# Turning the fifth and sixth chunk at other places, moving two decay tables, output copies of later groups on VectorE, and another order on GpSimd

## The chip, the cores and the metric

The kernel runs on one core of one Trainium2 chip. The metric is the device time of one execution in microseconds (us), here the median of several runs. Besides, one execution is taken by the hardware profiler; its span runs from the first to the last instruction, and its own run time is a little longer than its span.

The engines: TensorE (PE, with its weight loads as PEld), VectorE (DVE), ScalarE (ACT), GpSimd (POOL) and SyncE (SP). Each works through its own list of instructions in order. In this kernel POOL issues all loads that change type on the way (f32 in memory, bf16 on the core), and SP issues the transposing DMAs and the stores.

## The reference

`q`, `k` and `v` are [4 batches, 8 heads, 768 tokens, 64]. The first half is a recurrent retention layer, the second a feed-forward layer with the snake activation:

```python
for t in range(S):
    state = gamma * state + outer(k[:, :, t], v[:, :, t])
    y[:, :, t] = scale * (q[:, :, t] @ state)
x = y.transpose(0, 2, 1, 3).reshape(B * S, H * D)     # 3072 x 512
h = x @ w_in                                          # 512 -> 2048
g = h + sin(alpha * h) ** 2 / alpha
out = g @ w_out                                       # 2048 -> 512, f32
```

## The kernel before, in words

**Chunks and groups.** The 768 tokens of a batch are cut into 6 chunks of 128. A chunk's retention is a masked product of its own q, k, v plus q times the state that the chunks before left. The list `P` holds the 24 chunks in the order of work: first the first chunk of every batch (`e0` to `e3`, also P[0] to P[3]), then the five others of batch 0 (P[4] to P[8]), of batch 1 (P[9] to P[13]), and so on. Feed-forward work goes by groups of chunks: group 0 has four chunks (512 tokens), groups 1 to 10 have two (256 tokens). Group 1 is P[4] and P[5], group 2 is P[6] and P[7].

**Stages of a chunk.** q and k are needed with the head dimension on the partitions, so they are turned: by eight PE transposes and one copy (`stage_T`, L241, the copy at L249 on ACT or L251 on DVE), or by a transposing DMA on SP (`turn`, L253). `stage_A` (L259) makes the scores in the PSUM tile `pa` and masks them on DVE into `aT` (L269). `stage_M` (L288) multiplies the state (`s_bd`) and `aT` into `py`, and DVE writes `py` times a decay table `qg[:, c]` into the feed-forward input `xT` (L310). The table of the c-th chunk of a batch is made once by `decay_table(c)` (L213, DVE). `keep_S` (L283, ACT) copies the new state out of the tile `ps`. v is scaled by the decay of its place by `scale_v` (L133, the instruction at L137), on POOL for most chunks. Batches 1 to 3 take their chunks 1 to 5 from one long load each (`load_seq`: eight DMAs each for q, k and v, one per head), and do scores, mix and state in one go (`burst`, L398: PE lines L327, L337, L341, L354, L357, L366).

**Feed-forward slots.** A `Slot` (L411) is one 128-row piece of the hidden layer for a group (two pieces from group 1 on): PE fills `ph` (L425), ACT takes the sine (L428), ACT or DVE squares it (`sq`: L433 on ACT, L435 on DVE), and `add` (L438, L440 on DVE) writes the activation into `gT`. `ff_out` (L447, PE at L450) multiplies a finished piece of `gT` by `w_out` into the output tile `po`; after 16 pieces `take` (L455) copies `po` to `o_sb` (L462) and SP stores it (L463). The tile `o_sb` has three buffers.

**PSUM tags.** `ph`, `po` and some of the turned tiles share four buffers of the tag `mm`, given out in turn. A new tile waits until what read or wrote the buffer's last tile is done. `po` of group 0's first two token tiles has the tags `ps` and `ty`, of which there is one each; `pa` is a tag of its own with one buffer.

**What sets the order.** `tc.manual_schedule()` (L60): each engine's list is the order in which the source calls the operations. Group 0's slots (L594 to L667) are written out by hand, with the helper `F(ts, fs)` for output products of group 0's first two token tiles, and `fill(n)` for the next n output products of its other two. Then come POOL's loads and scalings (L670 to L698), then the rest of P[4] and P[5] (L700 to L708). From group 1 on, `phase` (L543) runs a group's eight slots: in slot n it makes the Slot and its square, does what the last attention step left over ("exit", "keep", "hand"), calls the attention work tied to (group, n) by `at` (L716), then `now.add()`, and then its share of the output products of the group before (four per slot; two in group 1). Attention bursts lie in slots 1 and 5 of groups 2 and later. An output tile is finished in slots 3 and 7.

Of the kernel before, what the change touches and what calls it, by code (L numbers as in the profile page):

```python
# [15 lines left out]
def kernel(  # L16
# [15 lines left out]
    nc = tc.nc  # L32
# [36 lines left out]
    def chunk_of(t, j):  # L69
        b, c = divmod(j, NCH)  # L70
        return t[b, :, c * C:(c + 1) * C, :].rearrange("h s d -> s h d")

    def load_chunk(j, names="qkv"):
        for name, src in (("q", q), ("k", k), ("v", v)):
            if name not in names:
                continue
            if name == "v":
                t = big.tile([128, H, D], BF16, name="vr", tag="vr", bufs=10)
            else:
                if ("qk", j) not in raw:  # L80
                    raw["qk", j] = big.tile([128, 2, H, D], BF16, name="qkr", tag="qkr", bufs=9)
                t = raw["qk", j][:, "qk".index(name)]
            nc.gpsimd.dma_start(out=t, in_=chunk_of(src, j))  # L83
            raw[name, j] = t

    def wide(j):
        return j >= NCH + 2 and j % NCH > 0

    def load_seq(bt, names="qkv"):

        cs = [c for c in range(NCH) if wide(bt * NCH + c)]
        nh = 2 * len(cs)
        if "q" in names:
            raw["seq", bt] = (big.tile([128, nh, 2, NP, D], BF16, name=f"qk_seq{bt}"),
                              big.tile([128, nh, NP, D], BF16, name=f"v_seq{bt}"))
        tqk, tv = raw["seq", bt]
        for name, src in (("q", q), ("k", k), ("v", v)):
            if name not in names:
                continue
            for h in range(H):  # L100
                r = slice(64 * (h // NP), 64 * (h // NP) + 64)
                o = tv[r, :, h % NP, :] if name == "v" else tqk[r, :, "qk".index(name), h % NP, :]
                nc.gpsimd.dma_start(out=o, in_=src[bt, h, cs[0] * C:, :].rearrange("(f i) d -> i f d", i=64))  # L103
        for i, c in enumerate(cs):
            j, f = bt * NCH + c, slice(2 * i, 2 * i + 2)
            raw["qk", j], raw["k", j], raw["v", j] = tqk[:, f], tqk[:, f, 1], tv[:, f]
# [26 lines left out]
    def scale_v(j, eng):  # L133
        t, by = raw["v", j], kg
        if wide(j):
            t, by = t.rearrange("i f p d -> i (f p) d"), kgq
        eng.tensor_mul(t, t, by[:, j % NCH, :, None].to_broadcast([128, H, D]))  # L137
# [74 lines left out]
    def decay_table(c):  # L212
        nc.vector.tensor_mul(qg[:, c], qg[:, 0], step[:, c, :, None].to_broadcast([128, NP, C]))  # L213
# [27 lines left out]
    def stage_T(j, eng=None, tag="ty"):  # L241
        pt = psum.tile([128, 2 * NP, 128], BF16, name="pt", tag=tag, bufs=4 if tag == "mm" else 1)
        st["qkT", j] = work.tile([128, 2 * NP, 128], BF16, name="qkT", tag="qkT", bufs=6)
        for i in range(2):
            for p in range(NP):
                nc.tensor.transpose(pt[:, i * NP + p, :],
                                    raw["qk"[i], j][:, 2 * p:2 * p + 2, :].rearrange("p h d -> p (h d)"), ident)
        if eng is nc.scalar:
            nc.scalar.copy(st["qkT", j], pt)  # L249
        else:  # L250
            nc.vector.tensor_copy(st["qkT", j], pt)  # L251

    def turn(j):  # L253

        st["qkT", j] = work.tile([128, 2 * NP, 128], BF16, name="qkT", tag="qkT", bufs=6)
        nc.sync.dma_start_transpose(out=st["qkT", j], in_=raw["qk", j].rearrange(
            "i a f p d -> i (a f p d)" if wide(j) else "i a h d -> i (a h d)"))

    def stage_A(j):  # L259
        qkT = st["qkT", j]  # L260
        pa = psum.tile([128, 2, NP, 128], F32, name="pa", tag="pa")
        for p in range(NP):
            for e in range(2):
                r = slice(64 * e, 64 * e + 64)
                nc.tensor.matmul(pa[:, e, p, :], qkT[r, NP + p, :], qkT[r, p, :],  # L265
                                 start=(p == 0), stop=True, skip_group_check=True)
        aT = work.tile([128, 2, NP, 128], BF16, name="aT", tag="aT", bufs=2)
        m = dec.rearrange("p e n t -> p (e n) t") if j % NCH == 0 else mask_bc
        nc.vector.tensor_mul(aT.rearrange("p e n t -> p (e n) t"), pa.rearrange("p e n t -> p (e n) t"), m)  # L269
        st["aT", j] = aT  # L270
# [12 lines left out]
    def keep_S(j, ps):  # L283
        for e in range(2):
            r = slice(64 * e, 64 * e + 64)
            nc.scalar.copy(s_bd[(j % NCH + 1) % 2][r, :, r], ps[r, :, :])  # L286
# [116 lines left out]
    def run(more, *kinds):  # L403
        for kind in kinds:
            if more and kind in more:
                more.pop(kind)()
# [37 lines left out]
    po = {}  # L444
# [10 lines left out]
    def take(g, ts):  # L455
        o_sb = work.tile([128, d_model], F32, name="o_sb", tag="o_sb", bufs=3)
        if (g, ts) == end:
            h = d_model // 2
            nc.vector.tensor_copy(o_sb[:, :h], po[g, ts][:, :h])
            nc.scalar.copy(o_sb[:, h:], po[g, ts][:, h:])  # L460
        else:
            nc.scalar.copy(o_sb, po[g, ts])  # L462
        nc.sync.dma_start(out=out_view[:, groups[g][ts], :], in_=o_sb)  # L463
# [79 lines left out]
    def phase(g, outs, att, nf=1, on_vector=()):  # L543


        no, done = len(outs), 0
        for n in range(FF // nf):
            more, fresh = rest[0], {}
            now = Slot(g, n * nf, nf=nf).sq("D" if n in on_vector else "A")
            run(more, "exit", "keep", "hand")  # L550
            for fn in att.get(n, ()):
                fresh.update(fn() or {})
            run(fresh, "mask")
            if fresh:
                rest[0] = fresh
            now.add()
            while done < no * (n + 1) * nf // FF:
                outs[done]()
                done += 1

    def T(j):
        return lambda: stage_T(j)

    def X(j):
        return lambda: turn(j)
# [7 lines left out]
    def SK(j):  # L573
        return lambda: keep_S(j, stage_S(j))
# [3 lines left out]
    P = order  # L578
    n3, n4 = 3 * C, 4 * C
    def F(ts, fs):  # L580
        for f in fs:
            for t in ts:
                ff_out(0, t, f)

    def early(f, tag="mm"):
        return Slot(0, f, (0, n3), tag=tag)
# [3 lines left out]
    def fill(n):  # L590
        for _ in range(n):
            outs.pop(0)()
# [10 lines left out]
    c = early(3)  # L603
# [11 lines left out]
    c = early(6)  # L615
# [24 lines left out]
    F((0, 1), (5,))  # L640
    a = Slot(0, 11)
    b.sq("D").add()
    decay_table(4)
    F((0, 1), (6, 7))
    b = Slot(0, 12)
    a.sq("A").add()
    decay_table(5)
    F((0, 1), (8,))
    a = Slot(0, 13)
    b.sq("D").add()  # L650
    F((0, 1), (9,))
    b = Slot(0, 14)
    a.sq("A").add()
    F((0, 1), (10,))
    a = Slot(0, 15)
    b.sq("D").add()
    F((0, 1), (11,))
    a.sq("A").add()
    stage_T(P[4], nc.scalar, "mm")
    F((0, 1), (12, 13))  # L660
    fill(2)
    stage_A(P[4])
    scale_v(P[4], nc.vector)
    F((0, 1), (14,))
    stage_T(P[5], nc.scalar, "mm")
    turn(P[6])
    F((0, 1), (15,))  # L667


    load_chunk(P[7])  # L670
    load_chunk(P[8], "qk")
    load_chunk(P[9], "qk")
    scale_v(P[6], nc.gpsimd)
    load_seq(1, "q")
    load_chunk(P[8], "v")
    scale_v(P[7], nc.gpsimd)
# [4 lines left out]
    scale_v(P[9], nc.gpsimd)  # L681
    load_seq(1, "v")
    scale_v(e2, nc.gpsimd)
    load_seq(2, "q")
    for j in P[10:12]:
        scale_v(j, nc.gpsimd)
    load_seq(2, "k")
    for j in P[12:14]:
        scale_v(j, nc.gpsimd)
# [7 lines left out]
        scale_v(j, nc.gpsimd)  # L697
    load_seq(3, "v")  # L698

    fill(1)  # L700
    stage_A(P[5])
    SK(e0)()
    scale_v(P[5], nc.vector)
    fill(5)
    stage_M(P[4])
    fill(4)
    stage_M(P[5])
# [8 lines left out]
    def at(place, fn):  # L716
        atts[place[0]].setdefault(place[1], []).append(fn)
# [8 lines left out]
    def B(old, new, first):  # L726
        return lambda: burst(old, new, first)

    at((1, 0), T(P[7]))
    for n in range(6, NJ + 1):  # L730
        new = P[n] if n < NJ else None
        first = new - 1 if n < NJ and new % NCH == 1 else None
        if n > 6 and wide(P[n - 1]):
            at(where[n], B(P[n - 1], new, first))
        else:
            if n > 6:
                at(where[n], lambda j=P[n - 1], last=wide(new): (M_last if last else stage_M)(j))
            at(where[n], lambda j=new: (scores if wide(j) else stage_A)(j))
            if first is not None:
                at(where[n], SK(first))  # L740
        if n + 2 < NJ:
            at(where[n], X(P[n + 2]))
        if n >= 19 and n < NJ:
            at(where[n], lambda j=new: scale_v(j, nc.gpsimd))
# [34 lines left out]
```

## Time and profile before

| | |
|---|---|
| median of 3 runs | 216.23 us (215.36 to 217.09) |
| the profiled execution: its time, its span | 216.35 us, 214.6 us |
| PE busy | 202.1 us (94%) |
| ACT busy | 167.6 us (78%) |
| DVE busy | 141.4 us (66%) |
| POOL busy | 107.2 us (50%) |
| granted PE clock | 1.00 throughout |
| ACT copies of output tiles, L462 | 23 of 0.571 us |
| POOL scalings, L137 | 21 of about 1.1 us |
| transposing DMAs of single chunks, from issue to landing | 8.6 us (median of 3) |

How to read it: a row of the timeline has the start, the length, the engine, the line, the operation, its tiles, and in brackets how long the engine had been idle and who ended that. A PE product's length is modelled to its end, and products overlap; the next product's start says more than the length of the one before. The list of waits adds up such idle times by pairs. The chain is followed back from the last instruction, at each step to what released it or to the instruction before it on its engine. The chain of this execution runs from the loads (POOL's issues, and DMAs of weights, q, k, v) over the scaling of `v_seq` at 81.50 us into PE, and stays on PE from 82.6 us to the last products.

### The profile page before, as it was taken

The page shows a single profiled execution, that of the slowest core. Times are in us where ns is not written, and L with a number is a line of the kernel's source. Part 1 is how long each engine was busy: PE and PEld are TensorE (multiplying, and loading weights), DVE is VectorE, ACT ScalarE, POOL GpSimd, SP SyncE. Part 2 cuts the span into 40 slices and gives each one's busy share as a digit, 9 for nine tenths or more (in the row PEclk, how much of TensorE's full clock was granted, in tenths as well). Part 3 has the DMA queues.
Part 4 walks back from the last instruction along what each step waited for, and adds up shares of the span by engine and source line. Part 5 has one row for each costly group of instructions (what it writes and reads, how often), then busy time and mean ns, then how long its engine had stood idle before and what let it go on. Part 6 is the DMA issues. An engine that isn't in the chain of part 4 may idle for free.

```text
span 214.6 us, 5482 instructions
## 1 busy us (share of the span) xinstructions
PE 202.1 (94%) x2171; PEld 134.5 (63%) x2197; DVE 141.4 (66%) x330; ACT 167.6 (78%) x365; POOL 107.2 (50%) x145
## 2 busy tenths in 40 slices
PE   7898899998999998999999999999999999999994
PEld 3444554456766666766766766666767667666654
DVE  4887859966896567477567568568576667555520
ACT  7688696757888986977977977977977877888841
POOL 8965433896879969999999500000330231000000
PEclk9999999999999999999999999999999999999999
DMA  9999999999998999999999913217304101100112
GB/s 130 150 194 186 206 207 169 154 127 216 160 139 72 153 175 188 157 130 200 164 124 169 151 33 101 73 25 101 93 11 101 49 3 50 52 28 21 49 53 98
DMA packets 101338, 25.01 MB, mean 117 GB/s; under 512 B 93872, under 2 KB 98368, under 8 KB 101312
## 3 DMA queue, kind: packets, MB, share of 16 engines
q0 software_dynamic: 77504, 13.38, 86.2%
q1 hardware_dynamic: 23664, 11.22, 24.8%
q8 instruction: 17, 0.28, 0.6%
q14 instruction: 9, 0.07, 0.1%
q10 hardware_dynamic: 144, 0.07, 0.1%
HBM read 27.27 MB, written 6.29 MB: 156 GB/s over the span
## 4 chain that ended last, share of the span: by engine, by line
PE 59%; DMA 25%; POOL 12%; issue 2%; DVE 0%; POOLq 0%; DVEq 0%
PE po L450 27%; PE ph L425 26%; DMA w_out<-in_moe_w_out_dram 8%; DMA w_in<-in_moe_w_in_dram 5%; DMA v_seq<-in_v_dram 4%; POOL qkr L83 4%; DMA qk_seq<-in_q_dram 4%; DMA qkr<-in_k_dram 4%; POOL v_seq L103 2%; POOL vr L83 2%; PE poh L473 2%; POOL vr L137 1%; PE py L327 1%; PE pa L337 1%; POOL qk_seq L103 1%
## 5 line engine op out<-in xcount | busy, mean ns | idle before, releaser
L440 DVE SCALAR_TENSOR_TENSOR gT<-s,rec_alpha,ph 128x256 bf16<-128x256 f32 (+3 forms) x184 | 82.2, 488 | 55.1 <-ACT s L433 54.7
L428 ACT ACTIVATE s<-ph,alpha_sb 128x256 f32<-128x256 f32 (+3 forms) x184 | 79.2, 480 | 28.8 <-PE ph L425 27.6
L425 PE MATMUL ph<-xT,w_in 128*128 128x256 bf16 (+3 forms) x735 | 98.6, 277 | 0.3 <-DVE gT L440 0.2
L450 PE MATMUL po<-w_out,gT 128*128 128x512 bf16 x344 | 90.3, 379 | 3.9 <-issue 3.2
L425 PEld LDWEIGHTS <-w_in 128*128 128x128 bf16 x736 | 70.5, 98 | 31.8 <-issue 2.8
L433 ACT ACTIVATE s<-s 128x512 f32<-128x512 f32 (+1 forms) x92 | 57.1, 621 | 2.5
L450 PEld LDWEIGHTS <-gT 128*128 128x128 bf16 x368 | 34.0, 98 | 26.4 <-issue 0.9
L391 POOL CAST s_bd<-s_f 64x256 bf16<-64x256 f32 x10 | 3.9, 394 | 50.3 <-DVE s_f L386 26.6
L103 POOL DMA_DIRECT2D qk_seq<-in_q_dram x24 | 17.1, 756 | 4.2 <-DMA v_seq<-in_v_dram 2.1
L103 POOL DMA_DIRECT2D qk_seq<-in_k_dram x24 | 17.0, 760 | 1.1 <-DMA qk_seq<-in_q_dram 0.9
L103 POOL DMA_DIRECT2D v_seq<-in_v_dram x24 | 17.1, 783 | 0.0
L137 POOL TENSOR_TENSOR v_seq<-v_seq,kgq 128x512 bf16<-128x512 bf16 x14 | 14.8, 1106 | 3.0 <-DMA v_seq<-in_v_dram 2.7
L462 ACT COPY o_sb<-po 128x512 f32<-128x512 f32 x23 | 13.0, 571 | 2.5 <-PE po L450 2.5
L346 DVE TENSOR_TENSOR aTw<-pa,maskq 128x768 bf16<-128x768 f32 x14 | 13.3, 949 | 0.0
L83 POOL DMA_DIRECT2D vr<-in_v_dram x10 | 9.3, 925 | 3.9 <-DMA w_in<-in_moe_w_in_dram 1.7
L492 PE MATMUL spare<-warm 128*128 128x512 bf16 x27 | 9.8, 487 | 1.3 <-DVE warm L156 1.2
L377 DVE TENSOR_TENSOR xT<-py,qg 128x256 bf16<-128x256 f32 x28 | 10.4, 414 | 0.0
L83 POOL DMA_DIRECT2D qkr<-in_k_dram x9 | 8.1, 899 | 4.6 <-DMA w_out<-in_moe_w_out_dram 3.3
L83 POOL DMA_DIRECT2D qkr<-in_q_dram x9 | 8.1, 897 | 3.9 <-DMA w_in<-in_moe_w_in_dram 1.7
L269 DVE TENSOR_TENSOR aT<-pa,mask 128x1024 bf16<-128x1024 f32 x6 | 7.3, 1217 | 0.7 <-PE pa L265 0.7
L137 POOL TENSOR_TENSOR vr<-vr,kg 128x512 bf16<-128x512 bf16 x7 | 7.5, 1091 | 0.1
L286 ACT CAST s_bd<-ps 64x256 bf16<-64x256 f32 x14 | 5.1, 361 | 2.2 <-PE ps L279 2.1
(92 smaller groups left out, 151.8 us busy)
## 6 DMA issues: line engine op xcount, KB each, us to landing
out_dram<-o_sb SPq DMA_DIRECT2D x23, 256.0 KB, 2.3
w_in<-in_moe_w_in_dram POOLq DMA_DIRECT2D x4, 512.0 KB, 11.7
w_out<-in_moe_w_out_dram POOLq DMA_DIRECT2D x4, 512.0 KB, 15.4
vr<-in_v_dram POOLq DMA_DIRECT2D x10, 128.0 KB, 6.9
qk_seq<-in_q_dram POOLq DMA_DIRECT2D x16, 80.0 KB, 5.6
qk_seq<-in_k_dram POOLq DMA_DIRECT2D x16, 80.0 KB, 3.6
v_seq<-in_v_dram POOLq DMA_DIRECT2D x16, 80.0 KB, 4.1
qkr<-in_q_dram POOLq DMA_DIRECT2D x9, 128.0 KB, 7.1
```

The source lines that it names most:

```text
L83: nc.gpsimd.dma_start(out=t, in_=chunk_of(src, j))
L103: nc.gpsimd.dma_start(out=o, in_=src[bt, h, cs[0] * C:, :].rearrange("(f i) d -> i f d", i=64))
L137: eng.tensor_mul(t, t, by[:, j % NCH, :, None].to_broadcast([128, H, D]))
L346: return {"mask": lambda: nc.vector.tensor_mul(aT, pa[:, :, 0:384].rearrange("p e (m t) -> p e m t", m=2), maskq[:, None, None, :].to_broa ...
L377: nc.vector.tensor_mul(x[:, 2 * b:2 * b + 2, :], py[b][:, 0:256].rearrange("p (m t) -> p m t", m=2), qg[:, c, 2 * b:2 * b + 2])
L425: nc.tensor.matmul(self.ph[:, m, :], w_in[:, i, f * 128:(f + 1) * 128], xT[g][:, i, self.lo:self.hi], start=(m == 0 and i == 0), stop=(i = ...
L428: nc.scalar.activation(out=self.s[:, m, :], in_=self.ph[:, m, :], func=ACTF.Sin, scale=alpha_sb[:, f:f + 1])
L433: nc.scalar.activation(out=self.s, in_=self.s, func=ACTF.Square)
L440: nc.vector.scalar_tensor_tensor(gT[self.g][:, f, self.lo:self.hi], self.s[:, m, :], rec_alpha[:, f:f + 1], self.ph[:, m, :], op0=ALU.mult ...
L450: nc.tensor.matmul(po[g, ts], gT[g][:, f, ts * C:(ts + 1) * C], w_out[:, f, :], start=(f == 0), stop=(f == FF - 1))
L462: nc.scalar.copy(o_sb, po[g, ts])
L492: nc.tensor.matmul(spare["ps"], warm[:, :128], warm, start=True, stop=True)
```

## The change

Six edits. (1) `take` copies the output tiles of groups 1 to 10 on DVE; those of group 0 stay on ACT, and the very last tile, which is copied in parts at L477 and L479, stays as it is. (2) In `phase`, `now.add()` stands behind the output products and not before them. (3) In group 0's last slots P[4] is turned one slot earlier, into a tile of the tag `pa`, its scores follow one slot later, and P[5] is turned before product 14; the `fill` calls and the scaling of P[4]'s v are placed anew. (4) `decay_table(4)` and `decay_table(5)` go from group 0's slots to slots 0 and 4 of group 1. (5) On POOL, P[6]'s v is scaled before the q and k of P[9] are loaded. (6) On POOL, P[10]'s v, the first of batch 1's long load, is scaled before the q of batch 2 is loaded, P[11]'s after it.

On PE no instruction is added or removed, only some in group 0's last slots change places. On ACT 19 copies go, on DVE 19 come.

```diff
@@ take
+        elif g > 0:
+            nc.vector.tensor_copy(o_sb, po[g, ts])
         else:
             nc.scalar.copy(o_sb, po[g, ts])
@@ phase
-            now.add()
             while done < no * (n + 1) * nf // FF:
                 outs[done]()
                 done += 1
+            now.add()
@@ group 0's last slots
     a = Slot(0, 11)
     b.sq("D").add()
-    decay_table(4)
     F((0, 1), (6, 7))
     b = Slot(0, 12)
     a.sq("A").add()
-    decay_table(5)
     F((0, 1), (8,))
...
     b = Slot(0, 14)
     a.sq("A").add()
-    F((0, 1), (10,))
+    F((0, 1), (10, 11))
+    stage_T(P[4], nc.scalar, "pa")
     a = Slot(0, 15)
     b.sq("D").add()
-    F((0, 1), (11,))
+    F((0, 1), (12,))
+    stage_A(P[4])
     a.sq("A").add()
-    stage_T(P[4], nc.scalar, "mm")
-    F((0, 1), (12, 13))
-    fill(2)
-    stage_A(P[4])
-    scale_v(P[4], nc.vector)
-    F((0, 1), (14,))
+    F((0, 1), (13,))
     stage_T(P[5], nc.scalar, "mm")
     turn(P[6])
+    F((0, 1), (14,))
+    fill(2)
     F((0, 1), (15,))
+    scale_v(P[4], nc.vector)
@@ GpSimd's order
     load_chunk(P[7])
     load_chunk(P[8], "qk")
+    scale_v(P[6], nc.gpsimd)
     load_chunk(P[9], "qk")
-    scale_v(P[6], nc.gpsimd)
     load_seq(1, "q")
...
     scale_v(e2, nc.gpsimd)
+    scale_v(P[10], nc.gpsimd)
     load_seq(2, "q")
-    for j in P[10:12]:
-        scale_v(j, nc.gpsimd)
+    scale_v(P[11], nc.gpsimd)
     load_seq(2, "k")
...
-    fill(1)
     stage_A(P[5])
+    fill(2)
     SK(e0)()
     scale_v(P[5], nc.vector)
-    fill(5)
+    fill(4)
     stage_M(P[4])
...
     at((1, 0), T(P[7]))
+    for c, n in ((4, 0), (5, 4)):
+        at((1, n), lambda c=c: decay_table(c))
```

## The prediction, as put on record

> **What bounds the kernel now.** I read the page first, then the waits of PE by stretch, then the chain, and last the timeline around each wait of PE.
>
> ```profile
> PE 202.1 (94%) x2171; PEld 134.5 (63%) x2197; DVE 141.4 (66%) x330; ACT 167.6 (78%) x365; POOL 107.2 (50%) x145
> PEclk9999999999999999999999999999999999999999
> ```
>
> PE is busy 94% of the span at full clock, and the change takes no product from it. So only idle time of PE can be won. Where it lies, for the stretch from 36 to 84 us (two lists, PE's products and its weight loads; the columns are total us, times, longest):
>
> ```profile
> PE pa L265 <- ACT qkT L249: 0.7, 2, 0.5
> PE pa L265 <- DMA qkT<-qkr: 0.5, 1, 0.5
> PE py L354 <- POOL v_seq L137: 0.4, 1, 0.4
> PE po L450 <- DVE gT L440: 0.2, 1, 0.2
> ...
> PEld L265 <- DMA qkT<-qkr: 0.7, 1, 0.7
> PEld L354 <- POOL v_seq L137: 0.5, 1, 0.5
> ```
>
> Four waits: for the copies of the turned P[4] and P[5], for P[6]'s transposing DMA, for P[10]'s scaled v, and for one `add`. After 84 us no such wait is left, but the chain shows a small regular one:
>
> ```profile
> 95.52 0.87 PE ph L425 x8
> 96.40 0.86 PE po L450 x4
> 97.26 0.98 PE ph L425 x8
> ```
>
> The third piece is 0.11 us longer than the first, though both are eight equal products. The timeline says why:
>
> ```profile
> 96.59 0.57 ACT L462 COPY o_sb<-po 128x512 f32<-128x512 f32 x1
> 96.71 0.87 DVE L440 SCALAR_TENSOR_TENSOR gT<-s,rec_alpha,ph 128x256 bf16<-128x256 f32 x2 [1.35 <-ACT s L433]
> ```
>
> ACT's copy of the finished output tile ends at 97.16 and the next `ph`, which gets that buffer, starts at 97.20. In the stretch 84 to 147 us the chain has eight such pieces, seven of 0.98 and one of 1.00: 0.90 us in all.
>
> Sums are against the profiled execution, 216.35 us (span 214.6 and 1.75 around it). It lies 0.12 us above the median, 216.23.
>
> **Part 1 and 2: output copies on DVE, `add` behind the products.** ACT loses 19 copies of 0.571 us (10.8 us), DVE gains 19. DVE's copy out of PSUM is not in the trace at this size; the nearest rows are the 128x256 copy at L720, 0.42 us (L720 in the timeline at 75.86), and the 128x512 product at L310, 0.69 us. I take 0.69, the same size: 13.1 us more on DVE, 141 to 154 of 214 us. The copy comes before the `add` of its slot in DVE's list, so it is seen against the row above: the tile's last product ends at about 95.5, DVE is idle from 95.4 to 96.7, the copy runs from 95.55 to 96.24 and still leaves the `add` at 96.71. At either price (0.42 or 0.69) it is done almost a microsecond before ACT's was, and the wait at 97.09 goes. Worth 0.90 us; bounds 0 (another release of that buffer is as late) and 0.90. A loss needs a copy longer than the 1.35 us of idle time that cover it; then `add`, and the buffers that it frees, come late. Moving `add` itself costs PE nothing, since in a slot the products of the group before do not read the `gT` that this `add` writes.
>
> [...]
>
> **Part 6: P[10]'s v scaled before batch 2's q is loaded.** POOL's row in the timeline:
>
> ```profile
> 80.78 0.71 POOL L103 DMA_DIRECT2D qk_seq<-in_q_dram  x1 [0.32 <-DMA v_seq<-in_v_dram]
> 81.50 2.05 POOL L137 TENSOR_TENSOR v_seq<-v_seq,kgq 128x512 bf16<-128x512 bf16 x2
> ```
>
> The last of batch 1's v lands at 80.49 by the trace; POOL then issues one more load (to 81.49), scales from 81.50 to 82.55, and PE, ready at 82.03, goes on at 82.61. With the scaling first it ends at about 80.5 + 1.06 = 81.6, before PE asks. That frees up to 0.57 us. Queued behind it on POOL: eight q issues of 0.71 us (81.6 to 87.3, before 73.4 to 81.5), P[11]'s scaling (to 88.4; PE asks at 90.6), eight k issues (to 94.1, before to 89.2), P[12]'s scaling (to 95.2; asked at 98.6). SP's turn of P[14] waits for that k, issued at 92.5 now and at about 97 to 98 then, with the store of 97.2 behind it; at 5.4 us like the next turn it lands by 103.5, and its scores are due at 106.4. Slack of 2 us or more everywhere, so I cost these at nothing; if the cover were gone PE would wait for the excess once.
>
> **Part 4: the two tables.** Each is 0.67 us of DVE (five at L213). Taken from 35.3 and 36.6, they let products 12 to 14 come earlier (part 3). Put into slot 0 of group 1, the first delays an `add` by 0.28 us and the mask of P[6] by 0.07: hidden. In slot 4 there is no room:
>
> ```profile
> 58.62 0.87 DVE L440 SCALAR_TENSOR_TENSOR gT<-s,rec_alpha,ph 128x256 bf16<-128x256 f32 x2 [0.28 <-ACT s L433]
> 59.41 0.68 DVE L435 TENSOR_TENSOR s<-s 128x512 f32<-128x512 f32 x1
> 60.13 0.87 DVE L440 SCALAR_TENSOR_TENSOR gT<-s,rec_alpha,ph 128x256 bf16<-128x256 f32 x2
> 60.92 0.68 DVE L310 TENSOR_TENSOR xT<-py,qg 128x512 bf16<-128x512 f32 x1
> 61.52 1.21 DVE L269 TENSOR_TENSOR aT<-pa,mask 128x1024 bf16<-128x1024 f32 x1
> 62.66 0.86 DVE L440 SCALAR_TENSOR_TENSOR gT<-s,rec_alpha,ph 128x256 bf16<-128x256 f32 x2
> ```
>
> DVE runs from 58.62 to 63.53 without a gap, and its last `add` there ends the wait of `po` at 63.57 (PE idle from 63.24). Of the table's 0.68 us, 0.28 fit into the idle time before 58.62; 0.40 reach that `add` and PE. Bounds 0 (PE has run ahead less) and 0.68. I take +0.40.
>
> **Part 3 and 5: P[4] and P[5], and P[6]'s v.** From 38.3 to 48.3 us PE waits about 1.1 us: 0.1 at P[4]'s turn, 0.2 at its scores, 0.6 at P[5]'s scores, 0.2 at the state. Worked out anew from rows: product 11 ends at 37.69; P[4]'s k lands at 38.03, so its turn ends at 38.3; Slot 15 to 39.16, product 12 to 39.6; the copy of 0.99 us from 38.5 lets the scores in at 39.6. Product 13 to 40.36; P[5]'s k lands at 40.91, its turn ends at 41.2, its copy at 42.4. Product 15 needs its `add`, now behind P[4]'s mask (1.22 us, from 40.4 to 41.6), so 42.35; scores of P[5] at 42.8; state from 43.7; `stage_M` at 45.06, where it is 45.03 now. New waits of 0.2 (k), 0.4 (k) and 0.35 (`add`), and one more change between product shapes (0.2), eat what is won. But this hardly matters: PE comes to P[6]'s scores at about 51.0 and waits until 51.51 for P[6]'s turn, issued at 43.73 when its k has landed and landed at 51.46. No edit moves that issue. What is won before it is lost there; up to 0.5 lost before it costs nothing. Bounds -0.5 (the turn lands that much earlier) and +0.3 (losses of 0.8). I take 0.
>
> POOL's scaling of P[6]'s v waits for its landing (44.53) and then takes 1.16 us, so P[9]'s q is issued at about 45.7, not 43.29, and batch 1's q at 47.4, not 46.23. Most of this is covered, as eight loads are in flight. I take 0 for the loads that follow; bound +1.2 us of lateness.
>
> **Sum.** At 82 us: PE comes 0.40 later (82.43) and finds v ready (81.6), so it is 0.18 ahead of 82.61. After that 0.90. 216.35 - 0.18 - 0.90 = 215.27, say 215.3.
>
> **Rivals.**
> - P[6]'s turn lands 0.5 us earlier, since P[9]'s loads are not yet beside it. For: it takes 7.7 us, the shortest turn 3.1. Against: its own issue stays, and other loads are queued. PE comes to 82 us at 81.93; the sum is -0.64 - 0.90 = 214.8. With the table's 0.40 hidden too, 214.4.
> - Slower: the whole load stream comes late, because POOL stands waiting for P[6]'s v. Lateness d shows where v of P[10] is scaled: ready at 81.6 + d. The point at which it eats all is 82.61 + 0.90 - 81.6 = 1.9 us. For: P[9]'s q is 2.4 us late. Against: batch 1's q is only 1.2 late, and the queue is full. At d = 2.4: 216.35 + 1.4 - 0.9 = 216.85.
> - The copies free nothing: `ph` waits as long for DVE. For: DVE takes the copies in order, and its square or mask may stand before them. Against: 1.35 us idle there. 216.35 - 0.18 = 216.2.
>
> **How the numbers follow.** Forecast 0.48, early turn 0.24, late loads 0.13, copies that free nothing 0.15. The range goes below 214.4 by the 0.5 that the table's and the turn's bounds leave, 213.9, and above 216.85 to 216.9. Within 1% (214.1 to 218.4) is about what a measurement of this kernel can tell from no change: its three runs spread over 1.7 us. Faster by more needs 2.2 us of the some 2.4 that all bounds give together: 0.10, from the early turn's tail and some of the forecast. Slower by more needs late loads beyond 3.5 us: 0.05. The rest, 0.85, is the same.
>
> **What would show it.** Right: no piece of 0.98 in the chain's `ph` after 84 us; copies at L462 on DVE that start when `po` is done; no wait of L354 for v. P[6]'s turn still awaited at 51.5. The wait of `po` for `gT` near 63.5 grown to about 0.6. Wrong: scores of P[6] well before 51, or waits at L303 or L354 for POOL; DVE's copies starting late, after a square; idle time of PE in batch 2's bursts from 106 us on.

## The result and the profile after

| | before | after |
|---|---|---|
| median | 215.86 us (8 runs, 215.18 to 217.09) | 214.41 us (8 runs, 213.81 to 215.42) |
| the profiled execution: time, span | 216.35, 214.6 us | 214.81, 213.0 us |
| PE starts P[6]'s scores (L265) | 51.51 us | 51.20 us |
| PE starts the `po` products that wait for `add` near 63 us (L450) | 63.57 us | 63.48 us |
| PE starts P[10]'s products of v (L354) | 82.61 us | 81.97 us |
| PE starts P[23]'s products of v (L354) | 185.90 us | 184.38 us |

The time is 0.9934 of before, 95% interval 0.9904 to 0.9963: about 1.4 us less. That is inside the 1% that the prediction called the same, though the interval does not reach 1. The two profiled executions differ by 1.54 us; the prediction's sum was 1.08. The rows of the table say where: 0.64 us until P[10]'s products of v, another 0.88 from there to P[23]'s.

The page of after, engines first. From L460 on its line numbers are higher by 2 (VectorE's copy is L462, ScalarE's L464, the store L465).

```profile
PE 201.3 (94%) x2171; PEld 134.3 (63%) x2197; DVE 155.1 (73%) x349; ACT 160.4 (75%) x346; POOL 107.2 (50%) x145
PE 72%; DMA 13%; DVE 7%; POOL 5%; issue 2%; POOLq 0%
```

VectorE has 13.7 us more; ScalarE has 7.2 less, not the 10.8 of its copies, since these overlapped their neighbours (in before the one at 96.59 by 0.20 us) and busy time counts that once; PE's share is as before. The second line is the head of the chain (followed back from the last instruction): VectorE now has 7% of it, in before 0%.

The chain of after in batch 2 (start, length, what), answering to the piece of 0.98 us shown for before:

```profile
93.02 0.87 PE ph L425 x8
93.89 0.86 PE po L450 x4
94.76 0.87 PE ph L425 x8
95.63 0.86 PE po L450 x4
96.49 0.87 PE ph L425 x8
```

And VectorE's timeline beside it:

```profile
94.79 0.69 DVE L462 COPY o_sb<-po 128x512 f32<-128x512 f32 x1 [0.19 <-PE po L450]
95.96 0.87 DVE L440 SCALAR_TENSOR_TENSOR gT<-s,rec_alpha,ph 128x256 bf16<-128x256 f32 x2 [0.47 <-ACT s L433]
```

The copy starts when the tile is finished, ends at 95.48, and the `ph` that takes its buffer, by the reading of before, starts at 96.33 without a wait. All pieces of `ph` in the stretch are 0.87.

The waits of PE's products between 36 and 84 us in after (us in total, times, longest):

```profile
PE po L450 <- issue: 1.3, 8, 0.2
PE pt L246 <- DMA qkr<-in_k_dram: 0.5, 1, 0.5
PE po L450 <- DVE gT L440: 0.4, 1, 0.4
```

Of before's waits, those for the copies of P[4] and P[5], for P[6]'s transposing DMA and for the scaled v are gone; a wait of 0.5 for P[4]'s k has come, and the one for `gT` has grown from 0.2 to 0.4. (The gaps marked "issue" are no waits; see the last section.)

The row of P[6]'s turn, in before and in after, by the view of DMAs of L256 between 42 and 46 us (the second line of each is the time from issue to landing):

```profile
L256 SPq DMA_TRANSPOSE qkT<-qkr x1: 1337/1337/1337, 43.7 to 43.7; - x1
...
DMA to landing us min/median/max: 7.7/7.7/7.7
```

```profile
L256 SPq DMA_TRANSPOSE qkT<-qkr x1: 1328/1328/1328, 43.9 to 43.9; - x1
...
DMA to landing us min/median/max: 5.4/5.4/5.4
```

It was issued 0.2 us later and landed 2.2 us earlier (49.30, not 51.46). And POOL's timeline ahead of P[10]'s products of v in after:

```profile
78.56 1.04 POOL L137 TENSOR_TENSOR v_seq<-v_seq,kgq 128x512 bf16<-128x512 bf16 x1 [5.48 <-ACT s L433]
79.55 5.76 POOL L103 DMA_DIRECT2D qk_seq<-in_q_dram  x8
```

POOL stood 5.5 us for the last of batch 1's v (landed 78.18, in before 80.49), scaled it by 79.6, and only then issued batch 2's q. The row names ScalarE as the one that ended the wait, but it was the load: POOL started 0.38 us after its landing here and 0.39 in early_act (landed 80.41, started 80.80).

### The profile page after: what moved, and what is told of

It is laid out like the page before. It is cut to its first block, busy times and chain, and to the rows that moved or that the text cites. A ratio compares the mean times of both kernels' runs of the same rounds, so it can differ in the third digit from the quotient of the medians.

```text
span 213.0 us, 5482 instructions
## 1 busy us (share of the span) xinstructions
PE 201.3 (94%) x2171; PEld 134.3 (63%) x2197; DVE 155.1 (73%) x349; ACT 160.4 (75%) x346; POOL 107.2 (50%) x145
## 4 chain that ended last, share of the span: by engine, by line
PE 72%; DMA 13%; DVE 7%; POOL 5%; issue 2%; POOLq 0%
PE po L450 32%; PE ph L425 30%; DMA qkr<-in_k_dram 8%; DMA w_in<-in_moe_w_in_dram 4%; DVE gT L440 3%; DVE aT L269 2%; POOL qkr L83 2%; PE poh L475 2%; PE pa L337 2%; PE py L327 1%; POOL vr L83 1%; PE py L366 1%; PE py L354 1%; POOL w_out L116 1%; PE py L299 1%
## 5 line engine op out<-in xcount | busy, mean ns | idle before, releaser
L450 PE MATMUL po<-w_out,gT 128*128 128x512 bf16 x344 | 90.5, 380 | 4.3 <-issue 3.3
L450 PEld LDWEIGHTS <-gT 128*128 128x128 bf16 x368 | 33.8, 98 | 27.0 <-issue 1.2
L462 DVE COPY o_sb<-po 128x512 f32<-128x512 f32 x19 | 13.1, 691 | 5.4 <-PE po L450 5.4
```

Source lines behind the costliest of these rows:

```text
L450: nc.tensor.matmul(po[g, ts], gT[g][:, f, ts * C:(ts + 1) * C], w_out[:, f, :], start=(f == 0), stop=(f == FF - 1))
L462: nc.vector.tensor_copy(o_sb, po[g, ts])
```

## The experiments

Twelve kernels, in three sets, each set on one chip with its own runs of before. Squares_beside, which changes the steady part itself, is left out of the table. One number sorts the others: the time from P[10]'s first product of v to P[23]'s (both L354), the steady part of the kernel, against the time up to it.

| kernel | of before, 95% interval | P[6]'s turn, us to landing | P[6]'s scores | P[10]'s v scaled | L354 of P[10] (waited) | to L354 of P[23] |
|---|---|---|---|---|---|---|
| before | | 7.7 | 51.51 | 82.56 | 82.61 (0.4) | 103.29 |
| after | 0.9934 [0.9904, 0.9963] | 5.4 | 51.20 | 79.61 | 81.97 | 102.41 |
| copies_only | 0.9957 [0.9926, 0.9988] | 8.0 | 50.98 | 79.64 | 82.44 | 102.40 |
| p10_first | 1.0004 [0.9972, 1.0035] | 7.8 | 51.26 | 80.88 | 81.81 | 103.27 |
| p6_first | 0.9971 [0.9950, 0.9993] | 5.5 | 50.99 | 80.21 | 81.53 | 103.28 |
| old_turns | 0.9926 [0.9899, 0.9953] | 5.6 | 50.98 | 78.35 | 81.53 | 102.40 |
| p9_first | 0.9931 [0.9904, 0.9958] | 8.1 | 51.17 | 81.41 | 82.03 | 102.41 |
| p10_back | 0.9911 [0.9885, 0.9938] | 5.6 | 50.82 | 79.92 | 81.59 | 102.41 |
| tables_early | 0.9898 [0.9867, 0.9930] | 5.6 | 51.28 | 80.37 | 81.83 | 102.41 |
| copy_add_ahead | 1.0137 [1.0108, 1.0166] | 5.5 | 50.83 | 78.71 | 81.71 | 107.13 |
| turns_tables | 0.9994 [0.9962, 1.0026] | 7.8 | 50.93 | 83.04 | 83.09 (1.2) | 103.32 |
| early_act | 0.9880 [0.9836, 0.9923] | 5.6 | 50.87 | 81.84 | 81.89 (0.4) | 102.43 |
| after_again | 0.9890 [0.9851, 0.9930] | 5.6 | 50.83 | 79.54 | 81.61 | 102.40 |

My theory after the result: the copies give their 0.9 in the steady part, and what is won before 82 us comes from the order on POOL, which lets P[6]'s turn land early, not from the new places of the turns. The rivals: the gain hangs together and cannot be taken apart, or the turning order carries it.

**The copies alone (copies_only).** Before, with these two edits:

```diff
+        elif g > 0:
+            nc.vector.tensor_copy(o_sb, po[g, ts])
...
-            now.add()
             while done < no * (n + 1) * nf // FF:
                 outs[done]()
                 done += 1
+            now.add()
```

> The kernel before with the output copies of the later groups on VectorE and add behind the products (parts 1 and 2), nothing else. Theory (the three gains are separate and add up): the pieces of 0.98 us of eight ph products after 84 us become 0.87, the wait for the scaled v at 82.6 us stays, and the span goes from 214.6 to 213.7 us (0.90 less). Rival (the whole gain of 1.5 us hangs on the order of POOL, and the copies only shift the wait): 214.3 to 214.6 us, with pieces of 0.98 or longer waits of PE for gT elsewhere.

Measured: 215.05 us against 216.01, profiled span 213.5. The theory holds for the steady part, 103.29 down to 102.40. The wait for the scaled v, which the theory expected to stay, was not there: in this execution v was ready at 79.64 in the old order. A new loss stood elsewhere, in the chain from 53 to 60 us:

```profile
53.20 0.47 ACT s L428
53.67 0.02 issue
53.70 1.99 DVE s L435
55.69 0.03 issue
55.71 0.87 DVE gT L440 x2
...
59.15 1.04 PE ph L425 x8
```

A square on VectorE took 1.98 us instead of 0.69, and the `ph` at 59.15 waited 0.9 us for it. POOL's timeline of the same kernel has the neighbour:

```profile
53.15 0.90 POOL L83 DMA_DIRECT2D vr<-in_v_dram  x1
54.07 1.05 POOL L137 TENSOR_TENSOR vr<-vr,kg 128x512 bf16<-128x512 bf16 x1
```

It is taken up under squares_beside.

**P[10] first, alone (p10_first).** Before, with `scale_v(P[10], nc.gpsimd)` ahead of `load_seq(2, "q")` and P[11]'s after it.

> The kernel before with one edit: P[10]'s v is scaled before batch 2's q is issued (part 6). Theory A (the last load of batch 1's v lands 2.3 us earlier, at about 78.2 us, because batch 2's q no longer runs beside it): scaled by 79.6 us, the wait of PE at 82.6 us goes, 0.57 us less, span 214.0 us. Theory B (that early landing comes from the other edits): landing 80.5 us as before, scaled by 81.6 us, the wait goes all the same, span 214.0 us. The landing tells them apart. Rival (what is queued behind it on POOL comes late): PE waits later for P[11]'s v or P[14]'s turn, span 214.6 us or more.

Measured: 216.19 us against 216.01, no gain; the interval reaches 0.6 us down, so a gain of 0.57 lies at its very edge. In the profiled execution, with 215.54 us one of the shorter ones, there was no wait of L354, as both theories had it. v was ready at 80.88, between A's 79.6 and B's 81.6, and its last landing is not on record, so this run does not tell the two apart. The span of 213.8 is 0.8 shorter than before's, but the median is not: the 0.57 us that the profile of before showed is not a gain that the median has.

**P[6] first, alone (p6_first).** Before, with the two lines of POOL exchanged:

```diff
-    load_chunk(P[9], "qk")
     scale_v(P[6], nc.gpsimd)
+    load_chunk(P[9], "qk")
```

> The kernel before with one edit: P[6]'s v is scaled before P[9]'s q and k are issued (part 5). Theory A (the two loads beside it slow P[6]'s transposing DMA): it lands at about 49.3 us, not 51.5, PE starts P[6]'s scores at about 51.0 us; the 0.2 to 0.5 us won there are lost again in a longer wait (0.8 to 1.1 us) for P[10]'s scaled v at 82.6 us, so the span stays at 214.6 us. Theory B (the early landing comes from the new place of the turns of P[4] and P[5], not from the loads): it lands at 51.5 us, the scores start at 51.5 us, span 214.6 us. The landing tells them apart.

Measured: 215.28 us, 0.9971 of before. Theory A is right on the landing, 48.91, 5.5 us after its issue, and the scores start at 50.99. Where it expected the gain to be lost again it was wrong: v was ready at 80.21, ahead of PE's 81.53, so the 0.5 us stayed. The times also lie closer together, 214.52 to 215.60, where before's 35 runs go from 214.47 to 217.87.

**The change without its turns and tables (old_turns).** After, with parts 3 and 4 undone.

> The kernel after, with the turning of P[4] and P[5] and the two tables put back as they were before (parts 1, 2, 5 and 6 alone). Theory A (P[6]'s turn lands early because of the order of POOL; the turning order cost 0.2 us and the table at 58 us held the add that PE waits for): scores of P[6] at about 51.0 us, the wait for gT near 63.5 at 0.2 us or less, no wait for v at 82 us, span 212.5 to 212.9 us against 213.0 after. Theory B (the new turning order brings the early landing): 214.6 less 0.90 less 0.57, span 213.1 us. Rival (turns and tables carry part of the gain): above 213.3 us.

Measured: 214.33 us, 0.9926 of before, span 212.6, as theory A had it. The new turning order and the moved tables are not what makes after faster.

**The turns and tables alone (turns_tables).** The reverse: before with parts 3 and 4 only.

> The kernel before with the new order of turning P[4] and P[5] and the tables in slots 0 and 4 of group 1 (parts 3 and 4), nothing else. Theory A (the parts add up: copies 0.9 less, P[6] first 0.6 less, P[10] first nothing, so 0.1 us is left for these two): within 0.3 us of before, P[6]'s turn landing at 50.8 us or later. Theory B (the table costs the 0.40 us that the prediction gave it at 63.5 us): 0.4 us longer than before. Rival (the new turning order carries part of the gain): 0.5 us or more below before.

Measured: 216.47 us against 216.44, 0.9994; no gain and no loss that the interval (0.8 us down, 0.6 up) can tell. P[6]'s turn took 7.8 us. In its profiled execution batch 1's v was late, last landed at 80.97, and PE stood:

```profile
PEld L354 <- POOL v_seq L137: 1.3, 1, 1.3
PE py L354 <- POOL v_seq L137: 1.2, 1, 1.2
```

So the wait that before's profile showed is real, but its size goes with when v lands: nothing in copies_only and p6_first, 0.4 in before, 1.2 here, all with the old order of P[10]. That the table costs 0.40 us (theory B) lies inside the interval and is not excluded by the time.

**P[6]'s scaling behind P[9]'s loads again (p9_first).** After with part 5 undone.

> The kernel after, with P[9]'s q and k issued ahead of P[6]'s scaling again (part 5 undone). Theory A (that order slows P[6]'s transposing DMA and puts GpSimd's scaling of P[7]'s v, which holds VectorE's square up, near 54 us instead of 55.3): P[6]'s turn lands at 50.8 us or later, PE loses 0 to 0.3 us at P[6]'s scores and, in some executions, up to 0.9 us at 58 us; median 0.5 to 0.9 us above after's, 215.0 to 215.3 us, and a wider scatter. Theory B (the prediction's: part 5 is worth nothing): same as after, 214.4 us.

Measured: 214.81 us, 0.9931. The turn took 8.1 us and PE stood 0.9 us for it. By the waits of PE between 36 and 84 us:

```profile
PE pa L265 <- DMA qkT<-qkr: 0.9, 1, 0.9
PE po L450 <- DVE gT L440: 0.5, 2, 0.4
```

The mechanism of theory A is there, but in time p9_first is between the theories: 0.4 us above p10_back of the same set, less than the 0.5 to 0.9 expected, and the intervals of the two overlap. In this execution PE had come early (P[5]'s scores at 42.13, in after at 43.11), so the wait cost only what was ahead.

**P[10]'s scaling behind batch 2's q again (p10_back).** After with part 6 undone.

> The kernel after, with batch 2's q issued ahead of P[10]'s scaling again (part 6 undone). Theory A (the landing of batch 1's v at 80.5 us in the profiled execution of before was a late one; v is ready by 79.6 to 80.2 us also in the old order, as in the runs with the copies alone and with P[6] first): PE asks at 82.0 us, waits for nothing, 214.4 us as after. Theory B (the prediction's step: v ready at 82.6 us in the old order): 0.57 us longer, 215.0 us, and a wait of L354 for the scaled v.

Measured: 214.40 us, no wait at L354, v ready at 79.92: theory A. With P[6] first, part 6 is worth nothing that these runs show.

**The tables where VectorE is idle (tables_early).** After, with both `decay_table` calls right behind `stage_M(P[5])`:

```diff
     stage_M(P[5])
+    decay_table(4)
+    decay_table(5)
     fill(4)
...
-    for c, n in ((4, 0), (5, 4)):
-        at((1, n), lambda c=c: decay_table(c))
```

> The kernel after, with both tables put right behind stage_M of P[5] (VectorE idle 48.3 to 50.0 us there) instead of into slots 0 and 4 of group 1. Theory A (table 5 at 57.9 us is what holds the add that PE waits for at 63.5 us): the gap of PE ahead of that po is 0.33 us or less instead of 0.56, nothing takes its place, median 0.2 to 0.4 us below after's, 214.0 to 214.2 us. Theory B (PE's other waits take it up: P[7]'s turn, v of P[10]): 214.4 us as after.

Measured: 214.05 us. The gap of PE ahead of that `po`, from start to start less the product's own time, is 0.33 us instead of the 0.56 that after, p9_first, p10_back and after_again have. Its chain from 59 us on has no table and no square held by one:

```profile
59.91 0.87 DVE gT L440 x2
60.78 0.60 DVE xT L310
61.38 1.13 DVE aT L269
62.51 0.79 DVE gT L440 x2
63.30 0.04 issue
63.35 1.02 PE po L450 x4
```

So the table costs PE 0.23 us there. Whether the time falls by it stays open: 214.05 (213.61 to 214.99) against 214.44 (213.66 to 214.72) for after_again on another chip, or 214.40 (214.03 to 214.87) for p10_back on its own, is no difference that six runs each can carry.

**`add` ahead of the products again (copy_add_ahead).** After with part 2 undone and part 1 kept.

> The kernel after, with add put back ahead of the products of the slot (part 2 undone, part 1 kept). Theory A (VectorE works its list in order, so the copy then stands behind an add that waits for ScalarE's square): the copy that began at 94.8 us ends after that add, 2 us later than now, and the next ph waits for its buffer 0.4 to 1.2 us for each of eight or more tiles: 218 to 230 us. Theory B (the place of add makes no difference, only the engine of the copy does): 214.4 us as after.

Measured: 219.35 us, 4.9 us above after and 3.3 above before. The waits of PE after 84 us:

```profile
PE ph L425 <- DVE gT L440: 3.2, 8, 0.4
```

The size is at the low end of theory A; from start to start each of the eight costs 0.56 us. What `ph` waits for is not the copy, as I had it, but the `add` itself. VectorE's timeline of this kernel, and PE's:

```profile
96.25 0.87 DVE L440 SCALAR_TENSOR_TENSOR gT<-s,rec_alpha,ph 128x256 bf16<-128x256 f32 x2 [1.36 <-ACT s L433]
97.04 0.68 DVE L462 COPY o_sb<-po 128x512 f32<-128x512 f32 x1
```

```profile
97.18 1.03 PE L425 MATMUL ph<-xT,w_in 128*128 128x256 bf16 x8 [0.39 <-DVE gT L440]
```

The `ph` that waits starts at 97.18, when this `add` has ended (97.12) and the copy has not (97.72); so it is at all eight. So this `ph` does not have the copied tile's buffer. Why it has another one here stays open: in before `add` stands ahead of the copy too, and there the `ph` at 97.20 started when ScalarE's copy was done (97.16) and the `add` was not (97.58). Part 2 is thus the condition for part 1; part 2 without part 1 was not run.

**A square beside a product of POOL (squares_beside).** After, with the squares of five slots of group 6 on VectorE and five idle products on POOL beside the last two (one for order, then five on the tile `warm`, which nothing reads any more):

```diff
-            now = Slot(g, n * nf, nf=nf).sq("D" if n in on_vector else "A")
+            now = Slot(g, n * nf, nf=nf).sq("D" if n in on_vector or (g == 6 and n in (2, 3, 4, 6, 7)) else "A")
+            if (g, n) == (6, 5):
+                nc.gpsimd.tensor_mul(warm[:, 0:256], warm[:, 0:256], gT[6][:, 8, 0:256])
+                for _ in range(5):
+                    t = warm.rearrange("p (h d) -> p h d", h=H)
+                    nc.gpsimd.tensor_mul(t, t, kg[:, 0, :, None].to_broadcast([128, H, D]))
```

> The kernel after, changed to measure one cost by itself: in group 6 VectorE does the squares of slots 2, 3, 4, 6 and 7, and from slot 5 on GpSimd runs five idle products of the size of its scaling of v (about 1.05 us each, on a tile of zeros that nothing reads). Theory A (a product of GpSimd stops a product of VectorE that reads and writes SBUF, and only that kind): the three squares without it take 0.69 us, those beside it 1.2 us or more, while add, mask and copies out of PSUM keep their 0.87, 0.95 and 0.69 us. Theory B (the 1.98 us of one square in the run with the copies alone had another cause): all squares take 0.69 us.

VectorE's timeline, a square with POOL idle, one beside POOL, and readers of PSUM beside POOL:

```profile
137.68 0.68 DVE L435 TENSOR_TENSOR s<-s 128x512 f32<-128x512 f32 x1
...
140.06 0.86 DVE L440 SCALAR_TENSOR_TENSOR gT<-s,rec_alpha,ph 128x256 bf16<-128x256 f32 x2
141.64 0.84 DVE L435 TENSOR_TENSOR s<-s 128x512 f32<-128x512 f32 x1 [0.72 <-ACT s L428]
142.40 0.74 DVE L377 TENSOR_TENSOR xT<-py,qg 128x256 bf16<-128x256 f32 x2
...
145.30 0.87 DVE L435 TENSOR_TENSOR s<-s 128x512 f32<-128x512 f32 x1 [0.98 <-ACT s L428]
```

And POOL's, the five idle products and the scaling behind them:

```profile
139.77 5.85 POOL L556 TENSOR_TENSOR warm<-warm,kg 128x512 bf16<-128x512 bf16 x5
145.58 1.49 POOL L137 TENSOR_TENSOR v_seq<-v_seq,kgq 128x512 bf16<-128x512 bf16 x1
```

Neither theory as written. Both squares beside POOL are longer, by 0.15 and 0.18 us and not by 0.5 or more, since each began near the end of a POOL product (140.89 to 141.93 and 144.58 to 145.62) and had only its rest to wait for: both end 0.55 us after it. The POOL products that came next were held in turn: one of the idle ones took 1.37 us and the scaling after them 1.49, against 1.04. The `add` at 140.06, which reads PSUM, kept its 0.86 in the middle of a POOL product. So here the two held each other up, by 0.15 to 0.45 us. (Its time, 217.92 us, is not compared: with the squares of slots 3 and 7 on VectorE the copies stood behind them, and PE waited for these twice, 2.7 us in all.)

**Early tables and ScalarE's squares (early_act), and after once more (after_again).** The first is tables_early with `phase(1, outs, atts[1], 2)` in place of `phase(1, outs, atts[1], 2, (2, 5))`.

> The kernel after, with both tables right behind stage_M of P[5] and the squares of slots 2 and 5 of group 1 on ScalarE instead of VectorE. Theory A (the squares on VectorE are what GpSimd's products hold up in some executions, and ScalarE has room): median 213.8 to 214.05 us, at most as long as with the early tables alone (0.9898 of before), slowest execution under 214.6 us. Theory B (ScalarE becomes what PE waits for between 53 and 63 us): waits of PE for ph or gT there of 0.3 us or more, 214.3 us or longer.

> The kernel after once more, for comparison with the others on this chip: 214.4 us, 0.993 of before, P[6]'s turn landed by 49.3 to 49.5 us, no wait of PE for the scaled v of P[10].

Measured: 214.24 us and 214.44 us on one chip, 0.988 and 0.989 of before. The two are the same. In early_act no wait for `ph` came, so ScalarE has room (theory B is out), but its slowest execution was 214.75, not under 214.6, and its profiled one had batch 1's v landing at 80.41, so PE stood 0.4 us at 81.9 although P[10] is scaled first. No version that I tried is faster than after by more than the runs can tell.

## Why the prediction was right, point by point

The time fell in the range, and on the side that was held likeliest. The sum of 1.08 came out as 1.54 in the profiled executions. That it came so near is in part luck: P[10]'s 0.57, which alone gave the median nothing, and P[6] first, which was put at nothing and alone gave 0.63, were off in opposite directions.

- **Copies and `add`, 0.90.** Right, in mechanism and size. The steady part is 103.27 to 103.32 us in all four kernels with the old copies, and 102.40 to 102.43 in the eight with the new pair of edits: 0.88 us. VectorE's copy took 0.691 us, where 0.69 was taken from a product of that size. That moving `add` costs PE nothing was right too, but too small a thing to say: left ahead of the products it would have cost 4.7 us in the steady part.
- **P[10]'s v, 0.57** (from start to start; 0.4 in the list of waits). Right for the execution that it was read from, and wrong as a term for the median. The wait is set by when batch 1's v lands, and v was scaled anywhere from 78.4 to 83.0 us in the thirteen executions of the table. Alone the edit gave 1.0004; undone in after, it changed nothing. The row "landed at 80.49" was one draw and I took it for a constant. The 81.6 was too early as well, as it left out the time from the landing to POOL's start: in early_act, with P[10] first and the landing at 80.41, POOL started at 80.80, v was ready at 81.84, and PE stood 0.4 us.
- **Tables, 0.40 at 63.5 us.** The place was right, the size not: 0.23, by the gap of 0.56 against 0.33 with and without the table. As the table's 0.68 us hit a VectorE that had begun a little earlier, with PE itself earlier by 0.3, the `po` started 0.09 us ahead of before's, where the prediction had it 0.40 late.
- **P[4] and P[5], 0.** Near enough: `stage_M`'s products of v came at 45.44 and not 45.28, with the new wait of 0.5 for P[4]'s k that was foreseen at 0.2. The 0.2 for a change between product shapes was an estimate of mine; in the chain of old_turns four `po` products take 0.97 us behind a burst's and 0.86 behind `ph`, 0.11 more. Turns and tables alone were 0.9994 of before.
- **P[6]'s turn, "landed at 51.46".** This is the step that failed. "No edit moves that issue" was true and did not matter: it is the landing that moved. In every kernel that issues P[9]'s loads ahead of the scaling (before, copies_only, p10_first, p9_first, turns_tables) the turn took 7.7 to 8.1 us, in every one that scales first 5.4 to 5.6. I had this as the first rival and gave it 0.24, with "its own issue stays, and other loads are queued" against it. That the order of the two on POOL moves the landing is shown, by that exchange alone (p6_first, p9_first). How the loads hold the turn up is not: in before P[9]'s two were issued 0.4 us before and 0.4 us after SP's turn, in after from 1.7 us after it on and in after_again from 1.95, and either way the turn had not landed yet. The early landing gave the profiled execution 0.31 us at 51 us, which the table then took up in part.
- **The late loads.** Did not come: batch 1's k was issued from 57.20 us on, in before from 57.47. The copies that free nothing: no wait of `ph` for them.

The 0.46 us between sum and measurement thus lie before 82 us: 0.31 from P[6]'s turn and 0.17 from the table, less 0.02 in the rest.

Set side by side, the parts alone give 0.93 (copies), 0.63 (P[6] first), about 0 (P[10] first) and 0.13 (turns and tables), by ratio times 216.0; that is 1.7 us against the 1.4 that after was measured at in its first runs and 2.4 in its second. The intervals of about 0.6 us on each do not allow a finer account. Two things stay open: how much of P[6] first is the turn and how much is that POOL's scaling of P[7]'s v then misses VectorE's square near 54 us, and how often that collision happens in before.

## What to carry to other kernels

A wait that shows once in a profile is worth its length only if its cause comes at the same time in each execution: where a DMA's landing sets it, as here (v was scaled at 78.35 to 83.04 us and PE waited 0 to 1.2), look at several executions before giving it a price. When a load is moved, price not only its own arrival but the transfers that were in flight beside it (P[6]'s turn took 7.7 us in before, 5.5 in p6_first). And when an operation that frees a buffer changes its place in the program, look anew at which operation each later tile waits for (in copy_add_ahead eight `ph` waited for `add`, 0.56 us each).

## What the runs showed of the hardware that I had not expected

- P[6]'s transposing DMA took 7.7 to 8.1 us from its issue to its landing in the five kernels where POOL issues P[9]'s two loads, which change type, ahead of P[6]'s scaling (in before 0.4 us before and 0.4 us after SP's turn), and 5.4 to 5.6 in the nine where it scales first (in after these loads came 1.7 us and 2.7 us after the turn): fourteen executions, no overlap.
- VectorE and POOL held each other up where both ran a product of two inputs that lie in SBUF. In after it is scaling beside scaling, VectorE's and POOL's timelines:

```profile
44.69 1.56 DVE L137 TENSOR_TENSOR vr<-vr,kg 128x512 bf16<-128x512 bf16 x1
```

```profile
44.66 1.04 POOL L137 TENSOR_TENSOR vr<-vr,kg 128x512 bf16<-128x512 bf16 x1 [1.06 <-DMA vr<-in_v_dram]
```

  VectorE's takes 0.68 us with no product of POOL beside it (at 42.43 in the same run). This one, the square of copies_only (1.98 us instead of 0.69) and the two of squares_beside (0.84 and 0.87) each ended 0.55 to 0.56 us after POOL's product. POOL's scaling in squares_beside (1.49 us instead of 1.04) ended 0.90 us after VectorE's square, at 147.07 and 146.17. Why one waits for the other these runs do not show, nor what settles which one does. Here the record of POOL's starts first, by 0.03 us, and VectorE's is the one that waited; but the square of copies_only began at 53.70, before POOL's product at 54.07, and yet it waited (POOL's took 1.05 us). What POOL did from 53.15 to 54.05 was to issue a DMA; whether that had a part in it is not tried.
- Some profiled executions lack records: after and before count 2171 products of PE where PEld counts 2197 weight loads, copies_only and old_turns count 2197 of both. The gaps of 0.2 us "issue" ahead of `po` are there only in the first kind; in the chain of after one reads

```profile
90.31 0.16 issue
90.47 0.81 PE po L450 x3
```

  where old_turns has four products and no gap:

```profile
89.75 0.13 PE py L366 x16
89.87 0.97 PE po L450 x4
```

  So these gaps are a product that was not recorded, and no time to be won.
